# Weight fetches moved from GpSimd's DMA queue to ScalarE's, with five idle products and a new instruction order, in a two-layer spectral-filter and gated-FFN kernel

## The chip, the cores and the metric

One NeuronCore of a Trainium2 chip runs the whole program. The metric is device time in microseconds (us), the median of several executions. One further execution is taken with the hardware profiler; all rows of the trace come from that one.

## The reference

Four blocks follow each other on `x` (1 x 2048 x 512, fp32): filter, FFN, filter, FFN, each with a layer norm before it and a residual add after it.

```python
def _A_ref(x, w_r, w_i):                       # spectral filter
    X = rfft2(x, axes=(-2, -1)) * (w_r + 1j * w_i)
    return irfft2(X, s=(S, D), axes=(-2, -1))
def _B_ref(x, w_gate, w_up, w_down):           # bilinear GLU, F = 1792
    return ((x @ w_gate) * (x @ w_up)) @ w_down
x = x + _A_ref(_layernorm(x), A_w_r, A_w_i)
x = x + _B_ref(_layernorm(x), B_w_gate, B_w_up, B_w_down)
x = x + _A_ref(_layernorm(x), A_w_r, A_w_i)
x = x + _B_ref(_layernorm(x), B_w_gate, B_w_up, B_w_down)
```

## The kernel before, in words

**Tiling.** `xs` keeps x in SBUF as 16 row tiles of 128 x 512. A layer (filter and FFN) has these stages. `fwd` takes the row statistics and multiplies each of the 16 tiles by a twiddle matrix scaled with 1/sigma (`tp`). `middle` runs 16 times (g = 0 to 15): sums and differences of features (`fs`), a product with the feature transform (`dp`, copied to `zs`), a product across rows (`zp`), the elementwise filter (`ys`), a product back (`vq`), and a copy into `E`. `inv` turns `E` back, tile by tile (`yi`, `yo`) and adds to `xs`. It needs all sixteen `vq`.

**The FFN** is done in fp32 precision by splitting each operand into a high part (float32r) and a low part, with three products for each (`mm3`). Gate and up products use a Strassen scheme: `unit` makes seven products (`gx`, `gy`, `gw`, `gz`, `gv`) of activation combinations `XA`, `XS` with seven weight combinations, and multiplies the results. There are 14 slices `ft` of the hidden dimension; weights of a slice lie in two SBUF tiles, `wt`, of three and four blocks (`PARTS`), each block 128 x 2 x 2 x 128 values, high and low. In three of the four half passes the down projection also uses seven products (`down`: `ex`, `ey`, `ew`, `ez`, `ev`) with weight forms `bf`; its operands `sf` are cast by ScalarE and their low parts made by GpSimd. The first half pass uses the plain form (`db`).

**Kept weights.** In the first half pass of layer 0 `weights` and `down_forms` build all combinations on ScalarE and GpSimd, and `store` writes them to scratch in device memory (`gu`, `dn`) by SP's queue. In the three later half passes `kept_weights` (line 706) and `load_forms` (line 879) read them back through `fetch` (line 340), which issues on GpSimd's queue: 72 transfers `wt<-gu` and 40 transfers `bf<-dn`.

**Other transfers.** SP's queue carries the inputs, the twiddles and the output. It also carries `by_memory` (line 658): a normed tile is transposed in blocks on VectorE (`zt`) and finished through device memory, four stores `turns<-zt` and one load `xf<-turns` each.

**What sets the order.** Every operation is recorded with `plan.op`, with its engine, a cost for planning, and the tiles it reads and writes. `Plan.order` (line 262) then issues all of them in an order that is written out in the file as a packed list, `ORDER`; `PLACES` gives for each rotating buffer which copy a tile takes. So each engine's queue is fixed by `ORDER`, engines run their queues in order, and semaphores are put in by the framework. Since all operations are recorded by one line, rows of the trace show L308; tiles tell them apart.

**Banks.** The eight PSUM banks are in rings `x` 1, `y` 1, `w` 1, `a` 3, `d` 2. `keep_warm` (line 512) is a product of `midt` with itself into a bank of ring `w` that nothing reads; two are recorded before the first `middle` of layer 0, and three before that of layer 1 (`IDLE`), between the last `tp` and the first `dp` by the key `"idle"`.

Of the kernel before, what the change touches and what calls it, by code (L numbers as in the profile page):

```python
# [28 lines left out]
def consts():  # L29
# [87 lines left out]
    '<w4$>uES&(y^7Ogofg5*g##b%WS$pfk+xv$!#rQCCuIUriY8(gS!;1gWt0j*|Ie}Ts=go#iF%4YBXgOlIUXs@O8UuC?JH{;VYrTvjy!u=RxwXanWJ-cy!_2ti{jZF;!=@VMDpGkd=Vy-'
    'S$_>?36n|siMVy$(~-Pgk$6?aKT)z%XW*^k@`^6`*Q)YZenTBf?r8$H4AFU#$=H!nOnT^ixrQB~c)tWFzoyOcVHnSgGor&=CUzH<r-)C4xE@_}C#~r^P*+HaAR`J&3tc9qiDV9|GxD@t'
    'u?n&-N_|<bO>|e#k|E`_h$$+q%`bi_bJdnITlGo2(+k{&%MwuDM3(8Jyb~@N_JVvW&thQ>y&y^EjIAeA)W^>~<qx8mLBE<>*rejgNkk(~zQ^Wr8fKCiGZ_yK2HPF+)D$pVPE(0@x`xO;'
    '(9%^_fSY|}nUQB$wdxw($JkA!EODzZZ*$#3R-15}U(;m1OtM*;VBD(S)B^mjNe12LtqRy4g3S@c`W$Fz#MR^AEmk(^er;@`^fI=j5&=)1k`F+7L+KzRwHi;FV|BJplr?1JYcfq+;{SK`'  # L120
    'aXBMH^j)6r!h0UMmQTh=6+BU%(N&Xmi5`bjX6hh$p1dC;N!s6hX)noE)>xUgu~M1$zR@=DLsPCQgQtV?8Ch(}=`&=;dELdEugWm#6WmpzR~UHjOHTE{mO0v$XwT7ab%Tr{_Yd-O1O#jY'
    'eMfYUz62^3X?ND%m-oI0+dFi-Ow<u(t(^&0j65OxOkdkiJ^^j{WwQ>I!#Y}KgXDTxGMo|f%h&Qce05Z}>QgYs%hF5}$@XlWjtyl&*H^53xJ+dY<;cj%`ig0%9hk8=a~fi*<Wr1%N|xS%'
    'Nfz49W}jZQCCnWn@<76|B1`W3L^gkz-@vbIdJvg@QVf16C@Ogx31i)cqjEub1YRh{xOZ6jcM^luj?avom6D+B3|Emnzol2DxZaS8MAM^h7*8U}n=IP8!M>-Zs>JJJo;Q@Gj8ei}v5{sE'
    'mKGs4`QSYxe@Y{A%~ciAl4dUvOC`_Kh{0JcqGioFdRKNe2VM*}S$dYaDye7AXay`PB!}@u8JMw}oaV`Ma?0j6=WQi(-=@I$?svFekxF><7@63V9F8X!Lb3fZ*rlua7^XO7|1yQN9HaDQ'
    '-Fx7}IiT-vJxv}S#d~R5MIXVo8q}OhuxpAw3-=t*npz7xLiILW(i}9jBr+#qoK$;I`hwnB+8@83wDnCMqf}yLw|Npx#QxMFAmDdab{GG<igAg|{L)5><-H1W+;%X|C+juS_AwXmK}Bjw'
    'EKj!K8CTCzK!=gpww!587NoP9J#h4LZ7Zd~%rff5cKf<Hs=LXkY2YkB78Qki7wI#2?=lsk8M9v33mQkfvg|GT*E8@OSH(2MC?oE(*O{v}<1fP7x%fYqoV$RBp2K%Zc&Rze(@lP6<rcdP'
    '4E{8|e_}<u$=n#K_bmEUk?*vXB!c(H$=@_$l>wrv!9LGY^=8<eW)Ys)3U6)29s>&1dh)V4#a##DdWH(Kff~AtIm$6=y8gus>D;C9-exk}p(395&d|1*k$c*`W)-z8m0av;J@3PyPg6XT'
    'tqtwRW|Tc^uEWcPseBh<fkzp2AwD{!pV=Qxe)uq54^q(w;O|a$nz^NKS-8bqgfpIH?Hz51cMjg^0?Qra_ph`X-uW9(_mUict?6Lrk?{q*ba=0uElBSNx&x-T1drC%*QLG9F@KY7b-`sc'
    'N-2$OZ7*f*2@_-Ud3XJB*qo32S;uNDKTdU2mUKTy&zU6ZSy^!zlI45MTTp6wtMwJT&BPOr$`WNSnzMc@$tPc#o)YQ3?oYKLjPSl`%{m{Uwmi(SlOX-H-_6_0OegetZ@zz&6||COGMe$@'
    '!G0V_9c1sB^?o-wXEu@%b3x5~oe8EQ><IIL6k_Dz=9hp+7s6B{sWWGE7I>c^tNb)A?IlPxnc?Sh^&F$k)KBFLKi*66U-Rbrjl501k(a%1{d`_?d~+VOu7qp$Q^(3;mD7P|u=NaROvZ!F'  # L130
    'si&L#1TT$Bwafp=d&4j0J@9LI#iSGHS}Co}CI2pMW4UW8seTOeT-Wm^Ru1}K(A$&t-a2OV^>c59=C?bvmFMBN4`qzsT<+o7vHr8(CI6yH_q%&>GRq(2z3or-R9Aw(^ZL8r&#Ob`Uf^zl'
    '-@|)Vn)z*|9b-m$7ySy}FaD=^`z!CD{^T34f$i@l!&p^hp6{}`rX+atSo;J2r1tWT`D)^b;WJW4+WYIg(>g~##O@dIevC9lH@5McvXXYeyVJZO{H=x#7~{RJ1?(X2XPto6(O!y%+dREz'
    's>%ibhQ8p1VVMEx9lVv~XiK!sRs5O{Zk!#|yT<Y>ez{MC8j$(vT3_Dv-}8!siZy;`R$?{AJL@<0+K}I&sEBR4-k;zZkn;nT=^&Wdh0PuC<xsB*b^o%S$7eNQfyPwW7s>GXy3k+g{RL+|'
    'VCJe=f13FdsdO>YLVh83Jx$%bS>9G{jV?Y(o<_n<7hw37@N=Z>hpA)HPP@T!X*i)aSj>PYQv(()LpA&ZJ#vmdam2*!368_+u`sq9v7|idU)DulG`>2)Xr%%zRgO$*#pqFTk&KOF#!Rqv'
    '0F;!$%BzfA3R}vN+a1Iy^)ghY0$lkh^V`%sMIlFt``Ls2+oU=fa)r5%gUsL6mo|*BQQYpp*Qa4upX#(yp44#PdMBxbUG-pIfshz@tUD2@MLleu7aFpe_Ef2=OW|!F{t09L&RAWSoWI4a'
    '_w#O%KbO!r{is+su{adZ=BL`vHv2W#jsh!#q^a&BCvWO|SkRdazDk_)gMchO#Qi14DT=KJq>Jvzs}vH=NcZrI)m2n!XYrQ2>LKOvURl}}OC0&OKCf-aB6%9M+!TFz9&J~RwY`J7xP)gi'
# [12 lines left out]
    ')E>k~wfWtG{_cD%ms*^I*RQdH%m7~p;FG_|uV&a+6OB|~w!`fQ=;7}E0Yg!=)Ri8nvpXPgtGWz*OC~XLC^!n0cC?km1J}8B{>UY3+<gZ)I~GiLXB?Mt`>CLZKxr*%#eI}bTP&$bwD##v'
    'eI6~9iRZ5|N<3bOAZpJAXKcwZOF?Y?ho>Lw40@c@o~VHm!AW2$J>9N2lguekuV`@yj1KVWP7E`NZzfh;;QeUk3&;Nn^a&?J+<9^&-0A$`v{6agOOnaaSbt63X>AVoj*)INQZyb86Nl()'  # L150
    'v>I6H5WX__HkSH4P`)P)2e>|{Px5yF<2Xz^1-glhFeszL+S`n=)j_NKxk+BfG2VXEZ38OMU~`h4remNGcz7UMYaP+KubbfEHQLW?vRANZ4r|ZAvxDj3)Yk;CvW*J5ksA3nI%p?~sJT=%'
    '-`RXrxhQrX<AS|Y5_P!`nA(jNZbMwUGl#Ex`CA`W91B)=aqUZ%y-(k@pm07`HzrFG@a1G3!|1(au{JYFpkO@nE(p|XJ{gA+9Zs(=u=X}R$H5ez6YtiJpIOcGU@uXAqUJlM8-jkBOG`Of'
    'q|PTjwG&$LC+$n`mFSP|tS*NqbJ#2QLc^}$eh>T=3S&67$b};^@WUnD&dz&bpv|6OUocI|1t%eU<rSXJB~pJ$BDqkWXboVU&&dL8ikInBqwg4ZH<@0Dn7;t4jgkRqx@6RYM_qr7*|!Gg'
    'LDBLaPaOUiGncZv83TG8PrCD53l}PEF$H}S36Hot=92%CJx|I^9ZJ;Pb4zV4L%cny7W8*#!gqpEsx!u!f6s{5NilV}IL&<7tm-B+6eSPJi>u}hS<z_NDP5zC2gin*0q7(zII&D;#~i5-'
    '&@5GhU6(r{zYSv+GEvOtqUTOKLuIv;C$m<fAnTx<ib#qKkbU-!USR&-D81A`am4DGfKdui*CHf=8t}NRV6U=MuSn&fZv-}E*jgx<!g8IJc<i1UXgjmfUdQtCu<So*(_8kUI2HOBW0fFN'
    'F0r53#oOia$u(wb%d_fo*WM#LTWdjco_JIPli#qH-$G<=Q;TBsYZUQ%Vp*ANKLeKc+Xxe_j_Izj?$(;k+@*<m1S7|Si*&N8vs|>5%(6gx=7Vcer~+%Kl!eI1kK`Xa3}j~LAP|ruX{^pw'
    ';+<I83I;N0CU>H_MXT#*GutjfE4C(^>q`Ul=`>>YbCA&qjJ=gO*V13G;2m~Y&GexLU4Tb&bRa7CD`^;<u-71pDOy}JP*$C=#B-X1OwYtiiRg%U?5${=Qfd#U#^ITbdcodcMG5fUUXVGI'
    'UhXRxd27p<Z0b-AkRDD|$f0eMW}!9R7mL=gaUB@(4;y7#!5q8Qo%m$fc=G@a=(N)<J#Gh?z5F)vs+npV7(<RPv@e)TcC+?3%K~lE4m7_fU)i!|j%{edgW9zL4^}nX)t&Vwu%dUVun%>X'
# [119 lines left out]
def kernel(ctx: ExitStack, tc: tile.TileContext, x, wf, wc, wb, dfwd, tf, ti, mid, out):  # L278
# [16 lines left out]
    def f32(ap):  # L295
        return ap.bitcast(F32)
# [34 lines left out]
    def pe(us, fn, r, w, **kw):  # L331
        return plan.op("PE", us, us, fn, r, w, **kw)
# [7 lines left out]
    def fetch(kb, fn, r, w, **kw):  # L340
        return plan.op("POOL", 0.6, 3.2, fn, r, w, kb=kb, **kw)
# [802 lines left out]
```

## Time and profile before

| | |
|---|---|
| median of 3 runs | 1079.55 us (1077.85 to 1081.14) |
| profiled execution, its own time | 1077.16 us |
| its span, first to last instruction | 1075.4 us |
| TensorE busy | 1052.6 us, 98% |
| VectorE busy | 817.4 us, 76% |
| GpSimd busy | 753.4 us, 70% |
| ScalarE busy | 406.0 us, 38% |
| moved by DMA | 193.65 MB, mean 180 GB/s |

PE is TensorE's matmul, PEld its weight load, DVE VectorE, ACT ScalarE, POOL GpSimd, SP SyncE. "A <- B" in a row of tiles is "A written from B"; in a row of waits it is "A waited for B". DMA issues are not counted as busy on SP and ACT, while GpSimd's transfers are shown in its rows as instructions with the time it takes to write their descriptors.

### The profile page before, as it was taken

The numbers are of one execution on the slowest core, as the hardware profiler recorded it, in microseconds if no ns is written. First come the engines' busy times: TensorE is split into PE (matmuls) and PEld (weight loads), VectorE is DVE, ScalarE is ACT, GpSimd is POOL, SyncE is SP. The second block draws the span as 40 slices with busy tenths as digits, with TensorE's granted clock in tenths as the row PEclk, the third lists the DMA queues.
The fourth block names the chain that finished last, engine by engine and source line by source line (L and its number), as shares of the span: only waits on it lengthen the run. The fifth ranks groups of instructions, "written<-read, shape, count | busy, mean of one in ns | idle before, by whom it ended". The sixth has DMA issues, their size and how long they took to land.

```text
span 1075.4 us, 18673 instructions
## 1 busy us (share of the span) xinstructions
PE 1052.6 (98%) x6546; PEld 907.4 (84%) x6546; DVE 817.4 (76%) x1603; ACT 406.0 (38%) x965; POOL 753.4 (70%) x1000
## 2 busy tenths in 40 slices
PE   8999999999999999999989999999999999999998
PEld 6677888887899888889967779888888998888897
DVE  7677876668976567777897688688788776677688
ACT  6458533334344223223354483222323431222321
POOL 6847698989999666677757038555678994566772
PEclk9999999999999999999999999999999999999999
DMA  9514346679744764656390004465877255565542
GB/s 361 228 40 177 109 172 222 229 258 296 220 173 170 255 219 158 205 164 220 102 368 1 3 14 141 164 216 157 248 223 220 83 169 209 205 208 175 196 147 79
DMA packets 84668, 193.65 MB, mean 180 GB/s; under 512 B 39264, under 2 KB 50784, under 8 KB 73568
## 3 DMA queue, kind: packets, MB, share of 16 engines
q0 software_dynamic: 16128, 102.77, 28.9%
q1 hardware_dynamic: 68160, 89.18, 24.1%
q8 instruction: 52, 0.85, 0.3%
q10 hardware_dynamic: 288, 0.52, 0.1%
q14 instruction: 40, 0.33, 0.1%
HBM read 145.52 MB, written 46.92 MB: 179 GB/s over the span
## 4 chain that ended last, share of the span: by engine, by line
PE 82%; DVE 5%; POOL 3%; issue 2%; ACT 2%; DMA 2%; SPq 0%; DVEq 0%; POOLq 0%; ACTq 0%
PE gx L308 13%; PE gz L308 13%; PE gw L308 7%; PE gv L308 6%; PE gy L308 6%; PE db L308 6%; PE ex L308 5%; PE ez L308 5%; PE dp L308 3%; PE zp L308 3%; PE yi L308 3%; PE ew L308 2%; PE ey L308 2%; PE ev L308 2%; PE vq L308 2%; PE yo L308 2%
## 5 line engine op out<-in xcount | busy, mean ns | idle before, releaser
L308 PE MATMUL gx<-xA,wt 128*128 128x512 f32 (+1 forms) x852 | 180.7, 347 | 1.9 <-ACT s L308 1.9
L308 PEld LDWEIGHTS gx<-xA,wt 128*128 128x128 f32 x852 | 137.2, 190 | 20.1 <-ACT s L308 2.1
L308 DVE TENSOR_TENSOR xs<-xs,db 128x512 f32<-128x512 f32 x128 | 85.2, 680 | 20.5 <-PE db L308 20.1
L308 POOL TENSOR_TENSOR sf<-cc,sf 128x256 fp32r<-128x256 f32 x103 | 76.1, 742 | 23.5 <-ACT sf L308 22.0
L308 PE MATMUL gz<-xS,wt 128*128 128x512 f32 (+1 forms) x426 | 91.0, 349 | 1.1 <-DVE q L308 1.1
L308 PE MATMUL db<-wd,h 128*128 128x512 f32 x336 | 91.0, 395 | 0.1
L308 PE MATMUL gy<-xS,wt 128*128 128x512 f32 (+1 forms) x426 | 90.5, 347 | 0.0
L308 PE MATMUL gz<-xA,wt 128*128 128x512 f32 (+1 forms) x426 | 90.2, 347 | 0.0
L308 PE MATMUL gw<-xS,wt 128*128 128x512 f32 (+1 forms) x426 | 89.9, 346 | 0.1
L308 PE MATMUL gv<-xS,wt 128*128 128x512 f32 (+1 forms) x426 | 89.9, 346 | 0.0
L308 POOL TENSOR_TENSOR sf<-q,sf 128x256 fp32r<-128x256 f32 x89 | 65.8, 741 | 32.3 <-ACT sf L308 31.8
L308 PEld LDWEIGHTS gz<-xS,wt 128*128 128x128 f32 x426 | 69.1, 189 | 12.0 <-DVE q L308 1.3
L308 PEld LDWEIGHTS gw<-xS,wt 128*128 128x128 f32 x426 | 69.5, 189 | 10.1 <-POOL xS L308 0.3
L308 PEld LDWEIGHTS gy<-xS,wt 128*128 128x128 f32 x426 | 68.9, 190 | 9.5 <-issue 0.5
L308 DVE TENSOR_TENSOR q<-gy,s 128x512 f32<-128x512 f32 (+1 forms) x71 | 41.0, 577 | 47.2 <-PE gy L308 28.3
L308 PEld LDWEIGHTS gv<-xS,wt 128*128 128x128 f32 x426 | 68.9, 190 | 9.4 <-issue 0.7
L308 PEld LDWEIGHTS gz<-xA,wt 128*128 128x128 f32 x426 | 68.8, 190 | 9.3 <-issue 0.5
L308 ACT COPY s<-gx 128x512 f32<-128x512 f32 (+1 forms) x71 | 35.1, 495 | 103.3 <-PE gx L308 95.1
L308 POOL TENSOR_TENSOR wt<-rg,wt 128x512 fp32r<-128x512 f32 (+1 forms) x56 | 64.2, 1157 | 13.0 <-ACT wt L308 12.8
L308 PEld LDWEIGHTS db<-wd,h 128*128 128x128 f32 x336 | 61.0, 188 | 12.8 <-DVE xs L308 1.0
L308 ACT CAST sf<-q 128x256 fp32r<-128x256 f32 x89 | 36.2, 406 | 87.6 <-DVE q L308 35.9
L308 POOL DMA_DIRECT2D wt<-gu x72 | 40.7, 565 | 34.9 <-PE gw L308 22.2
(163 smaller groups left out, 2557.3 us busy)
## 6 DMA issues: line engine op xcount, KB each, us to landing
wt<-gu POOLq DMA_DIRECT2D x36, 1024.0 KB, 5.3
wt<-gu POOLq DMA_DIRECT2D x36, 768.0 KB, 5.1
bf<-dn POOLq DMA_DIRECT2D x20, 1024.0 KB, 5.5
wq<-in_wf_dram SPq DMA_DIRECT2D x16, 1024.0 KB, 12.4
bf<-dn POOLq DMA_DIRECT2D x20, 768.0 KB, 4.7
gu<-wt SPq DMA_DIRECT2D x14, 1024.0 KB, 6.5
gu<-wt SPq DMA_DIRECT2D x14, 768.0 KB, 6.0
rg<-in_wb_dram SPq DMA_DIRECT2D x14, 512.0 KB, 4.4
```

Of the source, the lines that this page charges most:

```text
L308: ins = f(*args, **kw)
```

## The change

Four things are changed.

1. `fetch` issues on ScalarE's queue, and the planner's cost of it goes from 0.6 to 0.45 us. `kept_weights` and `load_forms` call `A.dma_start`.
2. The scratch of a weight part is laid out as [blocks, 128, 512] instead of [128, 2, blocks, 2, 128], and that of the down forms as [7, 128, 512] instead of [128, 7, 2, 256]. Store and fetch both go in pieces of 512 values (2 KB) for each partition, where a fetch had one piece of 6 or 8 KB for each partition.
3. `keep_warm` becomes `idle` with a key, a ring and a width, and five calls are new: one of 256 columns after the `vq` of g = 14 and one of 512 after that of g = 15, in each layer, ahead of the first `inv`; and one of 512 ahead of the `tp` of tile 14 in the second `fwd`. They write banks of ring `d`.
4. `ORDER` and `PLACES` are replaced.

```diff
@@ the packed order and places: replaced whole
...
     def fetch(kb, fn, r, w, **kw):
-        return plan.op("POOL", 0.6, 3.2, fn, r, w, kb=kb, **kw)
+        return plan.op("ACT", 0.45, 2.9, fn, r, w, kb=kb, **kw)
...
-        pe(0.9, spread, [*src, tw], [tp, *(["idle"] if t == 15 else [])])
+        if not tws and t == 14:
+            idle(1, "late", "d")
+        pe(0.9, spread, [*src, tw], [tp, *(["idle"] if t == 15 else []), *(["late"] if not tws and t in (11, 14) else [])])
...
-    def keep_warm(n):
+    def idle(n, key="idle", ring="w", cols=512):
         for i in range(n):
-            bk = bank("wp", "w")
-            pe(0.86, lambda bk=bk: TE.matmul(bk(), midt[:, 0:128], midt, start=True, stop=True), ["midt"], [bk, "idle"])
+            bk = bank("wp", ring)
+            pe(cols / 595, lambda bk=bk: TE.matmul(bk()[:, 0:cols], midt[:, 0:128], midt[:, 0:cols], start=True, stop=True), ["midt"], [bk, key])
...
-        pe(0.92, back, [y, "midt"], [vq])
+        pe(0.92, back, [y, "midt"], [vq, *(["turn"] if g > 13 else [])])
+        if g > 13:
+            idle(1, "turn", "d", (256, 512)[g - 14])
...
-        pe(0.9 if fold else 1.73, features, [*((E, "g", g, 0) for g in range(16)), di], [yi], due=early)
+        pe(0.9 if fold else 1.73, features, [*((E, "g", g, 0) for g in range(16)), di, *(["turn"] if t == 0 else [])], [yi], due=early)
...
-    kept = {(ft, i): dr.tile([128, 2, len(bs), 2, 128], F32R, name=f"gu{i}{ft}", tag=f"gu{i}{ft}")
+    kept = {(ft, i): dr.tile([len(bs), 128, 512], F32R, name=f"gu{i}{ft}", tag=f"gu{i}{ft}")
             for ft in range(14) for i, bs in enumerate(PARTS)}
-    kept_down = {p: dr.tile([128, 7, 2, 256], F32R, name=f"dn{p}", tag=f"dn{p}") for p in range(7)}
+    kept_down = {p: dr.tile([7, 128, 512], F32R, name=f"dn{p}", tag=f"dn{p}") for p in range(7)}
+    def pieces(t):
+        return t.rearrange("c p f -> p c f")
+    def rows(t):
+        return t.rearrange("p h b k f -> p (h b k f)").rearrange("p (c f) -> p c f", f=512)
...
-            fetch(262 * len(bs), lambda i=i: G.dma_start(ws[i](), kept[ft, i]), [("kept", ft, i)],
+            fetch(262 * len(bs), lambda i=i: A.dma_start(f32(rows(ws[i]())), f32(pieces(kept[ft, i]))), [("kept", ft, i)],
                   [(ws[i], hl, b) for hl in range(2) for b in bs])
...
-            store(262 * len(bs), lambda i=i: SP.dma_start(f32(kept[ft, i]), f32(ws[i]())), ...
+            store(262 * len(bs), lambda i=i: SP.dma_start(f32(pieces(kept[ft, i])), f32(rows(ws[i]()))), ...
...
-            fetch(256 * len(ms), lambda t=t, half=half, n=len(ms): G.dma_start(t()[:, 0:n], kept_down[p][:, 4 * half:4 * half + n]),
+            fetch(256 * len(ms), lambda t=t, half=half, n=len(ms): A.dma_start(f32(t()[:, 0:n].rearrange("p m h f -> p m (h f)")), f32(pieces(kept_down[p][4 * half:4 * half + n]))),
...
-        keep_warm(IDLE[layer])
+        idle(IDLE[layer])
```

The stores of the down forms (five kinds of call in `down_forms`) write `kept_down[p][m]`, whole rows of 512, in the same way.

More of the change, by code (lines that the diff above doesn't have):

```diff
@@ L117 @@
[L117 to L124, printed above, removed]
@@ new lines @@
+    'c-k$R2Y6OR*2mA>B#@BM0+Akygc?fdy$AxK7X<{ns4VJQmLeccM5KuFp@;=s7M0@Cq<18A2)%?BAoLC)1xW6k?>Coy^1SbR@7$R)r=S0s8<7Yx{6$KZ8p$IMG#?|6)RVmb`_9n^x=s?z'
+    'dHYCn)oQ4OOGC{x17)D~<Rx?7FCI|1sb!h{K*J<dE^09;Be$XWm=%TPzE+TH`a}z`&s`0dqT=g)cG|9WB_Ds6w22(jqGI))R$|5_jb-(-vR7-e!s=0I<d-l$_n_(MnSf>}_mNVF^;a}P'
+    's!53atufL>9<pmjuyY|f2HgnwDkoR;8QICIg8ZfHIjzOc*R+8wW=&zFEi9E}KclBKuT+#x`n;Ue1o(PZuES9SNz<xm=`dre7d4NRmOHv%tBEHi`8?3S^f@Uj|K>ZdT-AEaH^><wH?$zq'
+    'JV2I5aNsn0OK)g(Iji&aLuQ7dy@HaWA4_NLBe!%g^gW5wMN$V%8P<mL9VLz6=Onzw$a#&I1MqPG*)lX+%SdsqOG&(J<;hDjkzGg1$GS~hN_B~qeR@ahu)`g6p2VIh8Z8UeQ4g15XzPZ}'
@@ new lines @@
+    '?5j7i<)rNryglnluh9d}maumpxQ-0|PpFd&2KB#<)JD>Sw;YyPW2k4V7@Hc{Cp-9mq!QR@1-c(gJs3*w@djSlJUBy~A`ac;B|687>xIS!|5xNbV~Cjc@}-U>JFW>lsxg(!$@T~?Lx>2)'
+    'x2}VEBhgTIDs(F(i=;2hFTbPzn`D(A`E~vriPtV=)gN%=F|q->yo|ID0%X<@-QUJ@mf~UciM-ClSvXmuKH0bvbe*rZCGMR*o&(vmW~>*pTf@^*p7uxjmFyIceT!g$?nvU!AKm})EJq{9'
+    'vCk4M$v&sCfUoY|=KbI;Q3Rb<G%`Gc_e2M{IF@R99sQTXe=o2mm3)@1A;J6q;>^ub*9BK$N7a16NsN*I2V0+;6#')
+PLACES = (
+    '00000000000000000000000001230001121011302321304404010550500671086600107912170a000011001101052314007002800a3140100679005240800261900157000301'
+    '41907030a0001009500011640a0010390002460007054056a009003104a006800000002719000307100020006081121410004020701129223130046184110002270116800210'
+    '001140912500004335208790710001a041023140600804010009a010101200026010a0080300510000711001400600a101310600000710401600000003060071010604132010'
+    '10500004190001010031021001406013200001609014000120100001100000022410060110000091004003180100610001000200970603200401210071000610000007210601'
+    '70a10620301001110411279010000850216520001701800020301106170a00100101602071071200101800001100081020301040a010018010017900031000a0612000800911'
+    '00300a2072180000301690046117023089100201a06000074000001008a002807112004055233008440200011702021040720108000230306100a09602010204300600021103'
+    '100210540702540070001011837050040005012014030150402033001302124a0070310220090010092100a0132074000100301372108512006007410131000280a40006081a'
+    '003141028010071060301000a10005310840120301120010600132200150096413010018400051040330900840402101301a0600130716004020030601327100400412008310'
+    '70130401002121010803006491760101280040503100706129001110200701310642463706101001010112201171209716a00710750045000300630002108040a17051302060'
+    '9805013a409026120000a700101620a00700000164902001a002050900028a040006509000007400a11300005629002000101700250a10440211807013242606511090125200'
+    '701701a004011480023131000560040532009a00741108003050101a009623004200000070150090100223061004400710200190001510302408130a070401002056081300a0'
+    '4011004710000610050642019001030010632009051004112390410500012018005730002022003150301101a9205a0062103011000412900761503019007201042303200411'
+    '0a100104052700010041a0080400500731221a4043060020006540a0161054302018020004310410809030011001309004212350101140400879000760211308534001041601'
+    '20003101001201a000048052326a0011103081021009113040010221800090105413014070230208090045110320113400712006050101303200120090071046010003420000'
+    '001008063702020000114340008001120300251090314000803007120012918300050110010004001645001000600412340000a1720405000310018002115048030140103015'
+    '404300082108409001401001200041490007410240090310140011024000607a0341a00024900102010400705800019701230005100084023012040350003091807190205814'
+    '0010a0321004102010a418009420110100460010013491210087102000103a1451001209201040800061011001201')
@@ L744, in weights @@
         for i, bs in enumerate(PARTS):
-            store(262 * len(bs), lambda i=i: SP.dma_start(f32(kept[ft, i]), f32(ws[i]())), [(ws[i], hl, b) for hl in range(2) for b in bs],
+            store(262 * len(bs), lambda i=i: SP.dma_start(f32(pieces(kept[ft, i])), f32(rows(ws[i]()))), [(ws[i], hl, b) for hl in range(2) for b in bs],
                   [("kept", ft, i)], due=due + 3 * i)
@@ L754, in down_forms @@
         for m, j, n in ((0, 0, 0), (1, 1, 0), (4, 1, 1)):
-            store(256, lambda m=m, j=j, n=n: SP.dma_start(f32(kept_down[p][:, m]), f32(wd()[:, j, :, 256 * n:256 * n + 256])),
+            store(256, lambda m=m, j=j, n=n: SP.dma_start(f32(kept_down[p][m]).rearrange("p (h f) -> p h f", h=2), f32(wd()[:, j, :, 256 * n:256 * n + 256])),
                   [(wd, j, 0), (wd, j, 1)], [("down", p, m)], due=due)
@@ L763, in down_forms @@
         for n, m in enumerate((3, 5)):
-            store(256, lambda n=n, m=m: SP.dma_start(f32(kept_down[p][:, m]), f32(u()[:, n])), [(u, 0), (u, 1)], [("down", p, m)],
+            store(256, lambda n=n, m=m: SP.dma_start(f32(kept_down[p][m]).rearrange("p (h f) -> p h f", h=2), f32(u()[:, n])), [(u, 0), (u, 1)], [("down", p, m)],
                   due=due)
@@ L769, in down_forms @@
             pool(256, lambda n=n, u_=u_: gtt(u_()[:, 1], b(1, n), f32(u_()[:, 0]), ALU.subtract), [rws[1], (u_, 0)], [(u_, 1)])
-            store(256, lambda m=m, u_=u_: SP.dma_start(f32(kept_down[p][:, m]), f32(u_())), [(u_, 0), (u_, 1)], [("down", p, m)],
+            store(256, lambda m=m, u_=u_: SP.dma_start(f32(kept_down[p][m]).rearrange("p (h f) -> p h f", h=2), f32(u_())), [(u_, 0), (u_, 1)], [("down", p, m)],
                   due=due)
```

128 lines of the change are left out of this document (56 added, 72 removed).

## The prediction

> **What bounds the kernel now.** I read the page's head, then busy times cut into the kernel's stages, then what TensorE waited for, then the chain of work around its waits. The first fence has the span, the busy times, and one row for each stage (columns: stretch, busy us and instructions of PE, PEld, DVE, ACT and POOL, granted clock, DMA share, GB/s).
>
> ```profile
> span 1075.4 us, 18673 instructions
> PE 1052.6 (98%) x6546; PEld 907.4 (84%) x6546; DVE 817.4 (76%) x1603; ACT 406.0 (38%) x965; POOL 753.4 (70%) x1000
> ...
> core 0: us, PE busy (x) PEld busy (x) DVE busy (x) ACT busy (x) POOL busy (x), PEclk, DMA share, GB/s
> 0.00:75.00 75.00, 71.07 (x549) 51.79 (x549) 56.87 (x131) 42.28 (x96) 51.28 (x78) 1.00 0.55 215
> 75.00:80.00 5.00, 3.02 (x22) 2.59 (x21) 2.15 (x4) 2.58 (x5) 0.29 (x1) 1.00 0.45 157
> 80.00:340.00 260.00, 259.10 (x1358) 218.04 (x1357) 199.06 (x430) 118.85 (x266) 232.79 (x254) 1.00 0.60 204
> 340.00:540.00 200.00, 199.93 (x1289) 182.35 (x1289) 145.66 (x258) 59.83 (x158) 138.95 (x203) 1.00 0.58 189
> 540.00:565.00 25.00, 20.16 (x153) 16.27 (x151) 21.99 (x60) 12.55 (x39) 12.08 (x20) 1.00 0.90 357
> 565.00:604.00 39.00, 39.00 (x342) 27.92 (x341) 30.63 (x45) 20.42 (x35) 21.63 (x31) 1.00 0.00 1
> 604.00:637.00 33.00, 29.61 (x156) 22.57 (x155) 23.46 (x65) 20.06 (x50) 5.71 (x8) 1.00 0.04 13
> 637.00:770.00 133.00, 132.92 (x811) 117.27 (x810) 108.27 (x226) 45.75 (x118) 81.98 (x121) 1.00 0.53 166
> 770.00:826.00 56.00, 52.97 (x314) 46.26 (x313) 44.97 (x82) 15.73 (x38) 42.02 (x62) 1.00 0.81 243
> 826.00:1064.00 238.00, 237.78 (x1539) 217.09 (x1539) 176.29 (x294) 67.11 (x161) 165.66 (x226) 1.00 0.49 162
> 1064.00:1075.40 11.40, 7.07 (x33) 5.22 (x31) 8.05 (x17) 0.87 (x3) 0.98 (x2) 0.95 0.50 184
> ```
>
> TensorE is busy for 1052.6 of 1075.4 us, so all that a better order can win is 22.8 us, and the rows say where it lies. Stretch less PE busy: 3.93 in the first stage, 1.98 between the last `zp` and the first `yi` of layer 0, 0.90 in the first half pass, 0.07 in 340 to 540, 4.84 at the second `fwd`, 0 in its `middle`, 3.39 around the second `inv`, 0.08, then 3.03 in 770 to 826, 0.22, and 4.33 in the tail; together 22.8. Fetches run from about 340 to 1040. In 340 to 540, 637 to 770 and 826 to 1064 the sum is 0.37: there the products follow each other and nothing that GpSimd or ScalarE gains shows. Only 770 to 826, and the edge at 540, can answer to the move of the fetches. The granted clock is 1.00 everywhere but in the tail.
>
> What TensorE waited for, longest first (columns: us in total, times, longest):
>
> ```profile
> PE vq L308 <- DVE ys L308: 2.4, 2, 1.3
> ...
> PE gx L308 <- ACT s L308: 1.9, 1, 1.9
> ...
> PE tp L308 <- ACT rs L308: 1.7, 1, 1.7
> ...
> PE ez L308 <- DVE ew L308: 1.2, 1, 1.2
> ...
> PE gz L308 <- DVE q L308: 1.1, 1, 1.1
> ...
> PE yi L308 <- DVE mv L308: 0.9, 1, 0.9
> ...
> PE ew L308 <- ACT bf L308: 0.3, 1, 0.3
> ```
>
> `vq <- ys`, 2.4 us, are the two gaps at the end of each `middle`, a chain of VectorE that no fetch touches. `gx <- s` and `gz <- q` lie in 770 to 826. `tp <- rs`, `ez <- ew` and `ew <- bf` lie in 540 to 565, `yi <- mv` at the second `inv`.
>
> **The fetches leave GpSimd.** Its two groups (busy us, mean ns; then idle time just before them and what ended it):
>
> ```profile
> L308 POOL DMA_DIRECT2D wt<-gu x72 | 40.7, 565 | 34.9 <-PE gw L308 22.2 <-PE gz L308 7.6 <-PE gy L308 5.0
> L308 POOL DMA_DIRECT2D bf<-dn x40 | 22.9, 572 | 38.1 <-PE ew L308 20.9 <-PE ez L308 15.6 <-DVE cc L308 1.4
> ```
>
> That is 40.7 + 22.9 = 63.6 us of GpSimd's time, and up to 34.9 + 38.1 = 73.0 us more in which it stood before a fetch until TensorE had released the buffer. It goes off the path: GpSimd is busy for 165.66 of 238 us in 826 to 1064, and TensorE waits 0.22 there. By itself it is worth nothing but in the two stretches with gaps.
>
> **They enter ScalarE's queue.** What an issue costs there, and what transfers cost by queue (page: packets, MB, share of 16 engines' span; the others: min/median/max ns):
>
> ```profile
> q0 software_dynamic: 16128, 102.77, 28.9%
> q1 hardware_dynamic: 68160, 89.18, 24.1%
> ...
> wt<-gu POOLq DMA_DIRECT2D x36, 1024.0 KB, 5.3
> ...
> L380 ACTq DMA_DIRECT2D df<-in_dfwd_dram x1: 450/450/450, 1.2 to 1.2; - x1
> ...
> L308 SPq DMA_DIRECT2D turns<-zt x64: 569/627/2706, 188.5 to 817.5; - x64
> ...
> L308 SPq DMA_DIRECT2D gu<-wt x28: 327/467/1368, 93.1 to 331.9; - x28
> ```
>
> An issue of 128 pieces takes ScalarE 450 ns (`df`, one case; SP's stores of `gu`, 128 pieces too, 467). An issue with four times as many pieces is `turns`, 512 runs by its code, 627 ns on SP. The new fetch has three or four pieces for each of 128 partitions, so I take 0.6 us between 0.45 and 0.63: 112 x 0.6 = 67 us. ScalarE's busy time from 340 to 540 and 637 to 1064 is 59.83 + 45.75 + 15.73 + 67.11 = 188 us of 627; with 67 it is 255. The cover is its idle time:
>
> ```profile
> ACT s L308 <- PE gx L308: 95.1, 47, 6.7
> ...
> POOL wt L308 <- PE gw L308: 22.2, 4, 9.1
> ```
>
> It waits 95.1 / 47 = 2.0 us on average for `gx` before it copies `s`. A fetch of 0.6 us put there costs nothing. What is queued behind a fetch that waits for its buffer are the copies of `gx` and `ex` and the casts of `sf`; VectorE's `q` waits for `s`, GpSimd's low parts for `sf`, and TensorE for the single bank of `gx`. So a fetch costs TensorE time once it holds ScalarE for over about 2.0 us, that is 1.4 us of waiting beside 0.6. GpSimd's waits before `wt` show the danger: four of them for `gw` came to 22.2 us, the longest to 9.1. The order is new, so such waits on ScalarE can't be read off; I take 0, between 0 and +8 (the four waits less 2.0 each leave 14; half of that caught up).
>
> **Pieces of 2 KB.** From the queue rows: GpSimd's queue moved 102.77 MB in 28.9% of 16 x 1075.4 us, 20.7 GB/s for each engine with pieces of 6.4 KB; SP's 89.18 MB in 24.1%, 21.5 GB/s with pieces of 1.3 KB. Smaller pieces cost nothing for a byte, so the fetch of 1 MB stays at about 5.3 us. Fifty thousand packets come instead of 16128. The 28 stores of `gu` go from 467 ns towards 627 on SP, 28 x 0.16 = 4.5 us spread over 80 to 340, where TensorE idles 0.90; 0, bounds 0 and +0.6.
>
> **The gaps in 770 to 826.** Two, each behind a transfer:
>
> ```profile
> 769.13 1.10 POOL L308 DMA_DIRECT2D wt<-gu  x2 [0.50 <-PE gz L308]
> ...
> 769.58 7.50 DMA turns<-zt
> ...
> 777.26 0.60 ACT s L308
> 777.85 0.04 issue
> 777.90 1.66 PE gx L308 x6
> ...
> 824.28 0.42 DVE L308 TENSOR_TENSOR q<-gy,s 128x256 f32<-128x256 f32 x1 [2.17 <-DMA xf<-turns]
> ...
> 824.76 0.98 PE L308 MATMUL gz<-xS,wt 128*128 128x256 f32 x6 [1.13 <-DVE q L308]
> ```
>
> GpSimd issues two fetches at 769.13. A store `turns<-zt`, issued at 769.58, lands 7.50 us later; ScalarE can write `s` only then, and `gx` begins at 777.90 after 1.9 us of waiting. At 824.28 VectorE's `q` has waited 2.17 us for `xf<-turns`, and `gz` waits for it. So both gaps are late small transfers beside big fetches. After the change a fetch's piece takes a quarter as long, and the small pieces, if engines alternate between queues, come through sooner; but the bytes in front of them are the same. Also the order around these stores is another. Bounds: 0 and -3.03. I take -2.0, nearer to the gain, since only a landing about 2 us earlier is needed of 7.5.
>
> The rule that speaks against this stands in the Trainium skill, "DMA: Bandwidth & Descriptors", section "Issuing engines are not separate DMA queues": DMAs of all issuing engines interleave on the same 16 engines, and another issuer saves only its own issue time. By it alone this term would be 0; no run so far shows which holds.
>
> **The edge at 540.** `ew <- bf`, 0.3 us, hangs on a chain of GpSimd that loses its fetches; `ez <- ew`, 1.2 us, is VectorE doing two `st` ahead of `ew`, which an order can turn round or not. I take -0.6, bounds 0 and -1.5. Late next is `tp <- rs`, which stays.
>
> **Idle products.** Price of one of 512 columns from the three that layer 1 has already (start, us):
>
> ```profile
> 557.23 0.88 PE wp L308 x2
> ...
> 558.15 1.14 PE wp L308 x2
> ```
>
> 0.88 to 1.14 us. Five gaps take them: 1.3 and 0.7 us at the end of `middle` in layer 0 (1.98 together in the row 75 to 80), the like in layer 1, and 1.7 at `tp <- rs`. The product of 256 columns, half as long, fits the first; that of 512 after the last `vq` overshoots 0.7 by 0.2 to 0.4 in each layer; the one before tile 14 fits in 1.7. Cost +0.5, bounds 0 and +0.9. What they could bring is a clock that doesn't fall after a gap. In this execution it never fell (1.00 in each row), so the sum holds no gain; the lower bound is the 2.4 us by which the median lies above the profiled execution, if those are falls of the clock in the other ones.
>
> The Trainium skill, "TensorE: Matmul & The Clock Gate", section "HAM oscillation — how this bites in real kernels", puts the limit for idle gaps at about 3.4 us. The trace agrees so far: the longest wait here is 1.9 us and the clock stays at 1.00. By this rule no execution gains from idle products, and the 2.4 us of the median would stay: 1073.8 + 2.4 = 1076.2.
>
> **The new order** elsewhere: within reach are 0.90 in the first half pass, about 1.7 of the 3.39 around the second `inv` (the rest is the end of `middle`), and part of the 3.93 at the start. I take -1.3, bounds -4 and +3: a new order can open gaps in the 0.37 us stretches as well.
>
> **The sum** against the profiled execution, 1077.16: -2.0 - 0.6 + 0.5 - 1.3 = -3.4, so 1073.8. The runs' median, 1079.55, is 2.4 above that execution. I carry half of it: 1075.0.
>
> **The rivals.**
> - *The transfers are late anyway.* The 1.75 MB stay in front of the small stores, the order gives and takes, and the idle products cost what they cost: -0.6 + 0.5 gives 1077.1, with the 2.4 of the median 1079.4. For it: equal time for a byte; against it: only 2 of 7.5 us are needed. The rule of the Trainium skill on issuing engines, above, ends in this case.
> - *ScalarE is held at the head of its queue* (slower). Place: the fetches of `wt` and `bf` in 340 to 1064. Price: each microsecond over the 2.0 of slack stops `gx` for as long. With 8 fetches of 112 that hold ScalarE 1 us too long it is +8 on the case above, 1087.4; it decides, past +0.3%, from 4 such fetches. For it: TensorE ended 34.8 and 36.5 us of GpSimd's waits before its two kinds of fetch, and they now fall to ScalarE; against it: ScalarE idles for two thirds of these stretches.
> - *The order closes most of what is in reach*: 3.0 + 1.5 + 0.5 + 1.7 + 2 of the start = 8.7, with no cost of the idle products, and a median that comes down to the profiled value: 1077.2 - 8.7 = 1068.5.
>
> **How the numbers follow.** A measurement of this kernel can tell about 0.3%, 3.2 us, from no change. The forecast, 1075.0 (its own range 1071.5 to 1077.5), has 0.48, of which about 0.36 lies below 1076.3. Late anyway has 0.26, nearly all within 0.3%. ScalarE held has 0.15, of which 0.13 is beyond +0.3%. The closing order has 0.11. So faster 0.48, same 0.38, slower 0.14. The range 1068.5 to 1082.5 takes in all but the worse half of the held queue and a tenth beyond each end.
>
> **What would show it.** After the change, GpSimd's rows must hold no DMA; ScalarE's queue row must hold 112 issues of 0.45 to 0.63 us and some 102.8 MB. TensorE's waits must lose `gx <- s` and `gz <- q`, and the stretches that had 0.37 us of idle time must stay below 1. `turns<-zt` must land earlier beside fetches; if it doesn't and the gaps are gone, the order did it. Five more products of `midt` must lie in gaps, and the first `yi` of each layer may come 0.2 to 0.4 us later after its `vq`. The prediction is wrong if TensorE waits for ScalarE in the stretches that were full, or if the gaps at both layers' edges turn out to be what the new order closed.

## The result and the profile after

The changed kernel took 1071.74 us, median of 4 runs (1071.40 to 1072.81), against 1080.09 us of the kernel before measured beside it (1077.85 to 1081.14). The ratio is 0.9927, 95% interval 0.9909 to 0.9945: faster by 0.7%. Its profiled execution took 1071.40 us.

The head of the page after, then busy times cut into the same stages (boundaries moved with the work; columns as before):

```profile
span 1069.6 us, 18698 instructions
PE 1052.7 (98%) x6556; PEld 907.5 (85%) x6556; DVE 814.6 (76%) x1603; ACT 403.7 (38%) x965; POOL 691.0 (65%) x888
```

```profile
0.00:74.40 74.40, 70.41 (x551) 51.40 (x552) 55.59 (x132) 41.76 (x97) 50.84 (x78) 1.00 0.57 219
74.40:79.00 4.60, 3.60 (x23) 2.53 (x22) 2.06 (x3) 2.83 (x6) 1.51 (x2) 1.00 0.39 128
79.00:339.50 260.50, 259.09 (x1357) 217.97 (x1356) 200.42 (x431) 118.25 (x265) 229.91 (x251) 1.00 0.62 203
339.50:540.00 200.50, 200.50 (x1294) 183.00 (x1293) 144.49 (x257) 60.05 (x158) 119.47 (x167) 1.00 0.55 188
540.00:564.00 24.00, 20.80 (x155) 16.24 (x155) 20.92 (x60) 12.66 (x38) 11.40 (x20) 1.00 0.93 363
...
603.00:636.00 33.00, 30.66 (x168) 23.07 (x165) 23.83 (x66) 20.94 (x54) 6.39 (x10) 1.00 0.05 15
636.00:769.00 133.00, 133.00 (x813) 117.76 (x813) 109.43 (x228) 45.06 (x116) 67.96 (x96) 1.00 0.50 165
...
769.00:821.40 52.40, 51.72 (x310) 45.41 (x309) 43.89 (x80) 14.59 (x36) 34.79 (x50) 1.00 0.83 250
821.40:1058.20 236.80, 236.80 (x1537) 216.63 (x1536) 174.89 (x291) 66.08 (x161) 146.18 (x190) 1.00 0.49 165
1058.20:1069.60 11.40, 7.13 (x33) 5.26 (x32) 8.09 (x17) 1.29 (x4) 1.44 (x2) 0.98 0.49 184
```

TensorE's idle time fell from 22.8 to 16.9 us: 3.03 to 0.68 in the stretch that was 770 to 826, 4.84 to 3.20 at the second `fwd`, 3.39 to 2.34 around the second `inv`, 1.98 to 1.00 at the first (the new idle products count as busy there); the stretches that had 0.37 have 0; the first half pass went from 0.90 to 1.41. Most of the gain lies in the last FFN: from its first `gx` to its last `db` it took 432.97 us before and 428.76 after, 4.2 of the 5.8 us by which the spans differ. That is more than the 2.65 us of idle time lost between the first `gx` and the tail (3.03 + 0.22 + 0.08 less 0.68): the rest is not in idle time that the profile shows. Ends of products are modelled, so short stalls can lie inside "busy".

What TensorE waits for now, longest first (us in total, times, longest):

```profile
PE vq L308 <- DVE ys L308: 2.0, 2, 1.0
PE tp L308 <- ACT tws L308: 1.7, 2, 0.9
PE ez L308 <- DVE rs L308: 1.7, 2, 1.0
...
PE gz L308 <- DVE c L308: 0.7, 1, 0.7
```

`gx <- s`, `gz <- q`, `tp <- rs` and `ew <- bf` are gone. What is left in the last FFN is one wait of 0.7 for VectorE.

The queue rows and the fetch of 1 MB (median us from issue to landing), the new issues (min/median/max ns, first and last start), and the stores of `turns` that start between 740 and 830, the kernel before first, then the kernel after:

```profile
q10 hardware_dynamic: 52256, 103.29, 28.3%
q1 hardware_dynamic: 77120, 89.18, 24.8%
...
wt<-gu ACTq DMA_DIRECT2D x36, 1024.0 KB, 6.5
```

```profile
L308 ACTq DMA_DIRECT2D wt<-gu x72: 366/366/1072, 346.1 to 1026.5; - x72
...
L308 ACTq DMA_DIRECT2D bf<-dn x40: 366/366/526, 338.1 to 1032.4; - x40
```

```profile
L308 SPq DMA_DIRECT2D turns<-zt x24: 569/627/682, 745.0 to 817.5; - x24
...
DMA to landing us min/median/max: 2.2/3.3/9.6
```

```profile
L308 SPq DMA_DIRECT2D turns<-zt x24: 569/627/1061, 745.6 to 814.3; - x24
...
DMA to landing us min/median/max: 2.2/3.8/7.8
```

All 112 fetches are on ScalarE, at a median of 0.37 us each. The median store of `turns` lands no sooner (3.3 before, 3.8 after; the longest took 9.6 and 7.8). ScalarE still stands before one of them, with `yb` now and not `s`, and TensorE has other work meanwhile (engine line, wait in brackets):

```profile
781.00 0.37 ACT L308 COPY yb<-yi 128x256 f32<-128x256 f32 x1 [2.82 <-DMA turns<-zt]
```

### The profile page after: what moved, and what is told of

The parts are those of the page before. It is cut to its first block, busy times and chain, and to the rows that moved or that the text cites. A ratio compares the mean times of both kernels' runs of the same rounds, so it can differ in the third digit from the quotient of the medians.

```text
span 1069.6 us, 18698 instructions
## 1 busy us (share of the span) xinstructions
PE 1052.7 (98%) x6556; PEld 907.5 (85%) x6556; DVE 814.6 (76%) x1603; ACT 403.7 (38%) x965; POOL 691.0 (65%) x888
## 4 chain that ended last, share of the span: by engine, by line
PE 83%; POOL 6%; DVE 6%; DMA 2%; issue 2%; ACT 1%; SPq 0%; DVEq 0%; POOLq 0%; ACTq 0%
PE gz L308 13%; PE gx L308 13%; PE gw L308 6%; PE gy L308 6%; PE gv L308 6%; PE ex L308 5%; PE ez L308 5%; PE db L308 4%; PE dp L308 3%; PE zp L308 3%; PE ew L308 3%; PE yi L308 3%; PE ey L308 3%; PE ev L308 3%; PE tp L308 2%; PE vq L308 2%
## 5 line engine op out<-in xcount | busy, mean ns | idle before, releaser
L308 POOL TENSOR_TENSOR sf<-cc,sf 128x256 fp32r<-128x256 f32 x98 | 72.4, 742 | 65.4 <-ACT sf L308 57.5
L308 ACT CAST sf<-cc 128x256 fp32r<-128x256 f32 x98 | 39.2, 406 | 62.8 <-PE ew L308 21.3
```

Source lines behind the costliest of these rows:

```text
L308: ins = f(*args, **kw)
```

## The experiments

The change has three parts with a possible effect: the order, the queue of the fetches, and the idle products (the pieces are a fourth, inside the second). First each part by itself, and each taken back; then what it is in the queue that counts. The kernel before ran beside all of them, 85 executions in all with a median of 1079.55 us.

**The order alone.** The kernel before with `ORDER` and `PLACES` of the changed one, `idle("turn")` and `idle("late")` issuing nothing.

> The new order and places alone: fetches on GpSimd's queue with 6 and 8 KB pieces as before, and the five new idle products left out. If the order closed the gaps (theory A), about 1073.5 us or less, with no wait of TensorE over 0.8 us between 770 and 826. If earlier landings through ScalarE's queue and 2 KB pieces did it (theory B), 1078 to 1081, with waits for turns or xf again. If the idle products did it (theory C, the clock or the spread of the runs), 1074 to 1076: only the part that the profile shows.

Measured: 1080.87 us (1078.24 to 1082.56), ratio 1.0006 [0.9990, 1.0022]. The order alone gains nothing, and the first theory's 1073.5 us did not come. In its profile `gx <- s` and `gz <- q` are gone as in the changed kernel, but one wait stands in the stretch where they were, at 790.7 us, behind a late store of `turns`:

```profile
PE gz L308 <- DVE c L308: 2.4, 1, 2.4
```

So the order removes these two waits by itself, and the time does not follow. The clock fell twice for 3.4 us in this execution, behind the last `vq` of each layer.

**All but the order.** The changed kernel with the old order; five products put by hand into the gaps of the old order: 256 columns ahead of the last `vq` of each layer, 512 behind it, and 512 ahead of the `tp` of tile 12, not 14:

```diff
-ORDER, PLACES  (new)
+ORDER, PLACES  (old)
...
+            if not tws and t == 12:
+                idle_now(LATE, 512)
...
+            if BACKS[0] % 16 == 0:
+                idle_now(0, 256)
...
+            if BACKS[0] % 16 == 0:
+                idle_now(1, 512)
```

> Everything but the order: the queues of before, fetches on ScalarE's queue at their old places in the common order, 2 KB pieces, and five idle products put by hand into the gaps of before. Theory A: 1078 to 1081, the two gaps between 770 and 826 stay. Theory B: 1074 to 1077, those two gaps gone. Theory D (ScalarE is held at the head of its queue, since nobody arranged its order for this): over 1083, TensorE waiting for ScalarE in 340 to 540.

Measured: 1081.12 us (1076.30 to 1084.88), ratio 1.0010 [0.9992, 1.0027]. Both gaps of 770 to 826 are there, longer than before, and the clock fell to half behind each:

```profile
PE gz L308 <- DVE q L308: 3.7, 1, 3.7
PE gx L308 <- ACT s L308: 2.0, 1, 2.0
```

**The fetches alone.** As the last, without the five products: old order, fetches on ScalarE in 2 KB pieces.

> The fetches alone moved to ScalarE's queue with 2 KB pieces, in the order of before, no new idle product. Theory A: 1079 to 1081. Theory B: 1076 to 1078. Theory D: over 1083. If it stands within 1 us of the version with idle products, those bring nothing.

Measured: 1079.80 us (1076.25 to 1085.02), ratio 1.0006 [0.9989, 1.0023]. Its waits still hold those of 770 to 826:

```profile
PE gx L308 <- ACT s L308: 1.8, 1, 1.8
...
PE gz L308 <- DVE q L308: 0.9, 1, 0.9
```

So the queue by itself does not close these gaps, on which the prediction had put -2.0 us.

**The idle products alone.** The kernel before with the five products by hand.

> The kernel before with five idle products put by hand into its gaps: ahead of and behind the last vq of each layer, and ahead of the tp that waits at 551 us. Theory C (clock): 1076.5 to 1077.5 and a smaller spread of the runs. Otherwise 1079.5 to 1081, that is 0 to +0.9 us, by the products that overshoot their gaps.

Measured: 1081.96 us (1077.57 to 1083.64), ratio 1.0018 [1.0002, 1.0034]. In the old order they bring nothing; the ratio lies just above 1, and the 1.8 us more than the kernel before took beside it are past both ranges that were expected. They did stand in the gaps at the ends of `middle`. In the profiled execution the clock fell elsewhere, behind the wait of `gx` for `s`, here 2.4 us.

No part gains alone, and two of them without the order don't either. The next kernels take parts back from the changed one.

**Without idle products.**

```diff
-            pe(cols / 595, lambda bk=bk: TE.matmul(
+            pe(cols / 595, lambda bk=bk: key == "idle" and TE.matmul(
```

> The changed kernel without its five new idle products. The first four runs show the granted clock at half for 3.4 us behind gaps (1.7 us lost each time), in some executions and not in others. If the products are there to stop that at the ends of middle and the second fwd: median 1073 to 1076, spread 3 us or more, falls of the clock near 79 and 612 us in some executions. If they bring nothing (the view of the prediction): 1071 to 1072 with the same small spread.

Measured: 1073.71 us (1071.98 to 1074.14), ratio 0.9940 [0.9924, 0.9956]: 2.0 us of the gain are the idle products'. The spread, 2.2 us, is smaller than the 3 expected. The profile shows how. The stretch ahead of a fall of the clock and the two falls of this kernel, then its products at the first `inv` (start, us, idle time before in brackets), then the same place in the changed kernel:

```profile
75.00:78.50 3.50, 1.51 (x12) 1.16 (x10) 1.62 (x3) 1.73 (x5) 1.29 (x1) 1.00 0.43 157
78.50:81.90 3.40, 3.28 (x8) 2.65 (x9) 0.00 (x0) 0.89 (x3) 2.79 (x4) 0.50 0.00 0
549.60:553.00 3.40, 3.40 (x19) 3.40 (x18) 3.01 (x9) 1.15 (x5) 0.21 (x1) 0.51 1.01 426
```

```profile
74.77 0.61 PE L308 MATMUL vq<-midt,ys 128*128 128x128 f32 x4
76.81 1.13 PE L308 MATMUL vq<-midt,ys 128*128 128x128 f32 x8 [1.44 <-DVE ys L308]
78.62 1.22 PE L308 MATMUL yi<-di,E 128*128 128x256 f32 x2 [0.68 <-ACT E L308]
```

```profile
75.05 0.60 PE L308 MATMUL wp<-midt 128*128 128x256 f32 x2
76.65 1.13 PE L308 MATMUL vq<-midt,ys 128*128 128x128 f32 x8 [1.00 <-DVE ys L308]
77.62 1.02 PE L308 MATMUL wp<-midt 128*128 128x512 f32 x2
78.48 1.32 PE L308 MATMUL yi<-di,E 128*128 128x256 f32 x5
```

After idle times of 1.44 and 0.68 us the granted clock fell to 0.50 for 3.4 us. Half of it is 1.7 us, and from this `yi` to the first `gx` it took 27.3 us, against 25.7 in the changed kernel. With the products in place the longest single idle time there is 1.00 and the clock stays at 1.00. The first `yi` does not come later: the one of 512 columns overlaps its neighbours.

A fall does not follow such idle times each time. In this same execution 1.41 and 0.68 us at the end of the other `middle`, at 611, where a fall was expected, had none behind them; in the order alone the same two had one. The second fall here, at 549.6, came after waits of 0.68 and 0.97 us, which the changed kernel has as well (0.68 and 0.97) without a fall in its profile. The product ahead of tile 14 starts only at 552.95, behind that place, so what it does for the clock is not shown.

**The fetches back on GpSimd**, all else as changed.

```diff
-    A.dma_start(f32(rows(ws[i]())), f32(pieces(kept[ft, i])))
+    G.dma_start(f32(rows(ws[i]())), f32(pieces(kept[ft, i])))
...  (the fetch of the down forms in the same way)
```

> The changed kernel with its 112 fetches issued by GpSimd again, at the same places of the order, in 2 KB pieces, idle products kept. If the order needs GpSimd's freed time (theory E: order and queue only work together): 1075 to 1080, a wait of TensorE of over 2 us between 770 and 800, as with the order alone. If the queue is indifferent: 1071 to 1073.

Measured: 1081.94 us (1081.12 to 1084.04), ratio 1.0020 [1.0007, 1.0033]: the whole gain is gone, and more than the expected 1075 to 1080. With the new order, getting the fetches off GpSimd is worth 10 us at pieces of 2 KB (6.3 at the pieces of before, see further down); with the old one, from the pieces of before, nothing. Its GpSimd rows, and three of TensorE's waits from 340 to 560:

```profile
L308 POOL DMA_DIRECT2D wt<-gu x72 | 55.6, 772 | 19.4 <-PE gz L308 10.9 <-PE gw L308 5.0 <-PE gy L308 1.6
L308 POOL DMA_DIRECT2D bf<-dn x40 | 31.1, 779 | 28.1 <-PE ew L308 18.2 <-PE ez L308 7.9 <-PE gy L308 1.6
```

```profile
PE ex L308 <- POOL sf L308: 0.9, 1, 0.9
PE ez L308 <- POOL sf L308: 0.7, 1, 0.7
PE ew L308 <- POOL sf L308: 0.4, 1, 0.4
```

GpSimd makes the low parts of `sf`, and they come late. These waits do not add up to the 10 us: those for GpSimd's `sf` in the whole execution come to 2.6 us. Against the changed kernel TensorE's idle time is 4.8 us longer (21.7) and its busy time 5.6 (1058.3), so half of the loss is not named by any wait. Its place is seen better. From the first `ex` to the last `gx` of the second half pass it took 195.0 us here, 190.4 in the changed kernel and 192.4 with the order alone, at a clock of 1.00 in all three; from the first `gx` to the last `db` of the last FFN, 433.5 us against 428.8 and 432.4. An issue of pieces of 2 KB costs GpSimd 0.77 us, against 0.57 of pieces of 6 or 8 KB.

**Pieces of 6 and 8 KB on ScalarE**, all else as changed (old layout of `kept` and `kept_down`).

> The changed kernel with the scratch laid out as before: fetches on ScalarE's queue in pieces of 6 and 8 KB, stores in the same. If the small pieces let the small stores through sooner (part of theory B): 1074 to 1078, turns landing later beside fetches and a wait behind them. If the size of the pieces is indifferent, as the equal time for a byte says: 1071 to 1073.

Measured: 1071.99 us (1071.43 to 1075.38), ratio 0.9926 [0.9909, 0.9943]; the changed kernel run beside it (again below) took 1071.65. The pieces don't matter on ScalarE's queue. The 24 stores of `turns` landed after a median of 3.6 us, longest 9.6, as before. The profiled execution is the 1075.38: there one store came so late that TensorE waited 2.2 us for VectorE's `c`, and the clock fell after it. That dependence on a late store is still in the new order. It gave the 2.4 us of the order alone as well; in the changed kernel's profile the same wait is 0.7 us, and no store stands ahead of it.

**The changed kernel again.**

> The changed kernel as it is, on the chip of the three others, for its spread: 1071 to 1073, no fall of the clock between the start and the tail, gaps of TensorE all under 1.1 us.

Measured: 1071.65 us (1071.15 to 1072.84), ratio 0.9924 [0.9909, 0.9939]. In its profile the clock fell only at the very end, and the wait for `c` was 1.0 us.

**What it is in GpSimd's queue.** It is either the time of the issues, or that GpSimd stands before a fetch until its buffer is released. The changed kernel with other work at the 112 places, which waits for no buffer:

```diff
+    [G.memset(spare, 0.0) for _ in range(3)]
     A.dma_start(...)
```

> The changed kernel (fetches on ScalarE, new order, idle products), with three small memsets on GpSimd recorded at the place of each of the 112 fetches; nothing else waits for them. One memset of 128 columns takes 0.21 us in the trace, so three of 96 columns are an estimated 0.5 us, and 112 times that is 56 us of GpSimd's time, near the 63.6 us of its fetches in the kernel before. But they never wait for a buffer. Theory 'GpSimd's time': the new order needs the time that the fetches took there, and the gain goes: 1078 to 1082 us. Rival 'GpSimd's place in the queue': what hurt was GpSimd standing before a fetch until TensorE released the buffer (73 us in the kernel before); then the time stays at 1071.5 to 1074.

```profile
L308 POOL MEMSET spare<- 128x96 f32 x336 | 60.2, 179 | 13.4
```

Measured: 1077.47 us (1076.00 to 1080.71), ratio 0.9985 [0.9975, 0.9995]: 60.2 us of GpSimd's time cost 5.8 us, without any waiting for buffers (its busy time as a whole rose by 54, as spans overlap). The expectation's range, 1078 to 1082, was a little high.

The other half of the question is what fetches on GpSimd cost with short issues, order and idle products kept (the old layout):

```diff
-    A.dma_start(f32(rows(ws[i]())), f32(pieces(kept[ft, i])))
+    G.dma_start(ws[i](), kept[ft, i])
```

> The changed kernel with order and idle products kept, but fetches on GpSimd in the pieces of 6 and 8 KB of the kernel before (x1_order_alone with the idle products; x6_after_pool_fetch with 570 ns for an issue instead of 775). It tells GpSimd's time from its waiting. x9_pool_time gave GpSimd 60 us of other work at the same places without any waiting for buffers and took 1077.5 us. Theory 'GpSimd's time alone': here it is 64 us, so 1077 to 1079 us. Rival 'standing before a fetch until the buffer is released costs as well' (some 50 us of it in x1 and x6): 1079.5 to 1082 us, as x6, whose longer issues would then matter little.

```profile
L308 POOL DMA_DIRECT2D wt<-gu x72 | 40.8, 567 | 21.2 <-PE gz L308 11.5 <-PE gw L308 6.1 <-PE gy L308 3.0
L308 POOL DMA_DIRECT2D bf<-dn x40 | 22.9, 573 | 29.2 <-PE ew L308 18.6 <-PE ez L308 10.3 <-issue 0.2
```

Measured: 1078.03 us (1076.32 to 1080.29), ratio 0.9985 [0.9972, 0.9997]. With 63.7 us of issues and 50 us of standing before them it takes 6.3 us more than the changed kernel, the price of the memsets, which stood before nothing. In the second half pass, where the clock was 1.00 in both, the two agree most closely: from the first `ex` to the last `gx` 192.7 us with the memsets and 192.7 with these fetches, against 190.4 of the changed kernel. So GpSimd's time is what counts, about 0.1 us for each microsecond of it: 0, 60.2, 63.7 and 86.7 us of it gave 1071.7, 1077.5, 1078.0 and 1081.9. The last step costs more, 3.9 us for 23, and there the pieces are others too. What standing before a fetch adds is small but not bounded at zero: the executions at a clock of 0.999 or more, listed below, leave 1.2 us between memsets and fetches, which ran on different chips.

**The fetches on SyncE.**

```diff
-    A.dma_start(...)
+    SP.dma_start(...)
```

> The changed kernel with its fetches issued by SyncE, whose queue carries the stores of turns and the loads of xf beside them; all else as in the changed kernel. Theory 'off GpSimd is what counts': any queue that isn't GpSimd's does, and as a fetch that waits for its buffer holds back only other transfers here, 1071 to 1074 us. Rival 'it is ScalarE's place in the order that counts, and a fetch that waits on SyncE delays the small stores and loads behind it': 1075 to 1085 us, with new waits for turns or xf in the layer-1 FFN.

Measured: 1072.03 us (1071.24 to 1074.06), ratio 0.9933 [0.9919, 0.9948]. ScalarE's and SyncE's queues do equally well; small stores behind the fetches did not suffer (`turns` landed after a median of 2.8 us, longest 5.1).

**More work on ScalarE**, two copies of 96 columns ahead of each fetch:

```diff
+    [A.copy(spare, midt[:, 0:96]) for _ in range(2)]
     A.dma_start(...)
```

> The changed kernel with two copies of 96 columns on ScalarE ahead of each of the 112 fetches. By the copies of 256 and 512 columns (370 and 586 ns) one is an estimated 0.24 us, so a fetch holds ScalarE for 0.37 + 0.48 = 0.85 us, more than twice as long, 53 us in all. Theory 'ScalarE has idle time where the fetches stand' (it waits 2 us on average for gx): 1071 to 1073 us. Rival 'ScalarE is near its limit at the fetches': each 1 us of it shows in part on TensorE, 1075 to 1090 us.

```profile
L308 ACT COPY spare<-midt 128x96 f32<-128x96 f32 x224 | 60.8, 271 | 9.2 <-PE ew L308 2.6 <-ACT spare L308 1.0 <-PE gw L308 0.7
```

Measured: 1072.56 us (1072.29 to 1073.75), ratio 0.9938 [0.9926, 0.9950]: 60.8 us more on ScalarE cost 0.9 us, where 60.2 on GpSimd cost 5.8. ScalarE has the room, GpSimd does not.

**The clock in all executions.** The mean granted clock is listed with each execution. Of the 85 of the kernel before, 19 with 0.999 or more average 1077.7 us, 31 with 0.998 average 1079.1, and 35 below that 1081.5. A fall like those above, 3.4 us at half, takes 0.0016 off the mean. Executions at 0.999 or more, set side by side, hold hardly any falls:

| order | fetches | idle products | us at a clock of 0.999 or more (executions) |
|---|---|---|---|
| old | GpSimd | no | 1077.7 (19) |
| old | ScalarE | no | 1077.5 (3) |
| old | GpSimd | by hand | 1079.4 (4) |
| old | ScalarE | by hand | 1077.6 (3) |
| new | GpSimd, 6 to 8 KB | yes | 1077.6 (8) |
| new | GpSimd, 2 KB | yes | 1082.1 (9) |
| new | ScalarE, memsets on GpSimd | yes | 1076.4 (5) |
| new | ScalarE, 2 KB | yes | 1071.8 (9) |

So 5.9 us come from order and queue together, and about 2 more from the clock: its mean was 0.998 or less in 66 of 85 executions before, in all 6 without idle products, and in none of the 9 of the changed kernel. Where it fell in the kernel before is not known, since its only profile shows no fall ahead of the tail.

## Why the prediction was right, and where it was not

The forecast, 1075.0 us and faster, held in sign, and 1071.74 lies in its range. It was 3.3 us too high, and three of its steps failed.

**"By itself it is worth nothing but in the two stretches with gaps."** Right as far as it goes: with the old order the fetches alone changed nothing. It failed as a term of the sum, because order and queue were added as if they were independent. The old order gains nothing from a GpSimd that is free; the new one gives back on GpSimd what it gains, 5.8 to 10 us of it, and only off GpSimd keeps it. The busy times of after read 119.47 us of 200.5 on GpSimd in the second half pass, where nothing waits; with the fetches on it, `sf` is late. An engine that is busy for 70% of the span had, in the new order, no room where it was needed. How the lost time reaches TensorE is shown in part only: the waits for `sf` name 2.6 of the 10 us.

**"The gaps in 770 to 826", -2.0 us.** The size was near (3.03 to 0.68), the cause was wrong. The median transfer lands no sooner, the pieces make no difference, and with the old order both gaps stayed. The prediction had named this test itself: the gaps are gone and `turns` lands no earlier, so the order did it; with the order alone both waits are gone too. That the size came near is luck: the wait for `c` that took their place was 0.7 us in this profile and 1.0, 2.2 and 2.4 in others of the new order. The rule of the Trainium skill that it weighed against the term ("DMA: Bandwidth & Descriptors", section "Issuing engines are not separate DMA queues": another issuer saves only its own issue time) agrees with the runs: fetches from ScalarE and from SyncE took the same time. What the rule calls small, the issuer's own time, was worth 6 us here.

**Idle products, +0.5 us with a bound of -2.4.** Mis-sized with the wrong sign: -2.0 measured. In the changed kernel the first `yi` shows no cost, while by hand in the old order the time rose by 0.2%; and the falls of the clock that the bound allowed for were real. The sum had read a clock of 1.00 from one execution (its 0.95 in the tail was a fall, too late to matter), which is among the quarter of the kernel's executions that hardly have a fall. For the same reason half of the 2.4 us between median and profile was carried; in the changed kernel it is 0.3. By the Trainium skill ("TensorE: Matmul & The Clock Gate", section "HAM oscillation — how this bites in real kernels") gaps up to about 3.4 us do no harm, and idle products would gain nothing. The runs differ: the clock fell after idle times of 1.44 and 0.68 us, in some executions and not in others. The measurement decides.

**The edge at 540, -0.6 us.** `ew <- bf` went as said. `tp <- rs`, 1.7 us, which the prediction let stand, went too, and `ez` still waits for VectorE (1.7 us in two waits, 1.2 in one before). The stretch lost 1.6 us of idle time, just past the bound of 1.5, but an idle product fills part of it. From the last `gx` of the second half pass to the first `dp` it took 25.3 us before and 24.2 after; 24.4 with the order alone, and 25.3 with the fetches alone. So 1.1 us were gained, 0.9 of them by the order, where the term had named the freed GpSimd first.

**The new order elsewhere, -1.3 us.** Near: 0.98 and 1.05 us of idle time at the ends of `middle`, partly filled by idle products, and 0.37 in the full stretches, less 0.51 given back in the first half pass. The start, put down as in reach, kept its idle time (3.93 and 3.99).

**ScalarE's issues at 0**, right: 0.37 us for an issue, below the 0.45 to 0.63 taken, and 60.8 us more on top cost 0.9. The rival of the held queue did not come about. **Pieces of 2 KB at 0**, right for ScalarE; on GpSimd they would have cost 3.9 us (1081.94 against 1078.03). The fetch of 1 MB did not stay at 5.3 us from issue to landing; it takes 6.5 (6.1 in pieces of 8 KB), and no wait for it is among TensorE's.

The rival "transfers are late anyway" was right about the transfers and wrong about the time. "The order closes most of what is in reach" came as near in time as the forecast (3.2 us off), yet would have had the order do it alone.

## What to carry to other kernels

Parts of a change that each do nothing alone can gain together: a fixed order suits one load of each engine, so a freed engine can show only once the order is another. Before costing an operation at nothing because TensorE does not wait there, ask whether that stays true in the new order; work added to the engine at the same places, once with and once without its waits, tells time from waiting. A profile of one execution can miss what most executions have: compare the granted clock listed with each before taking the profiled clock as the kernel's.

## What the hardware showed that was not expected

- The granted clock fell to 0.50 for 3.4 us after idle times of 1.44 and 0.68 us close together; with products of 256 and 512 columns in them it did not. It is not certain to fall: 1.41 and 0.68 us were followed by a fall in one execution and by none in another, a single 2.24 by a fall and a single 2.38 by none.
- An issue of 384 or 512 pieces took ScalarE 0.37 us, one of 128 pieces 0.33; on GpSimd 0.77 and 0.57 us. So the larger number of pieces cost GpSimd 0.2 us an issue, ScalarE 0.04.
